# Operands kept in PSUM until they are split, upper halves on ScalarE, three norms in a row, unread matmuls, and a second product taken row by row

## The chip, the core and the metric

The kernel runs on one core of a Trainium2 chip. TensorE (PE) multiplies matrices and writes its results to PSUM, VectorE (DVE) and ScalarE (ACT) read and write SBUF and PSUM, GpSimd (POOL) works on SBUF alone, and SyncE's queue (SP) issues all the transfers of this kernel. Every engine takes its instructions in an order that is fixed when the program is built. The metric is the device time of one execution in microseconds (us); less is better.

## What is computed

For 8 sequences of 4224 positions with 192 channels, each position first gets a weighted sum of the last 7 positions, with weights from a softmax that is given per position and head (8 heads of 24 channels). Then comes the real part of a two-dimensional Fourier transform, a normalisation, and a two-layer network with 768 hidden channels:

```python
w = softmax(weight_gen, axis=-1)                      # 7 taps per position and head
u0 = sum over k of w[..., k] * x_padded[position + k] # dynamic convolution
u  = u0 + real(fft(fft(u0, axis=1), axis=2))          # mixing over positions and channels
un = (u - mean(u)) / sqrt(var(u) + 1e-6)
out = u + relu(un @ w_ch1) @ w_ch2                    # 192 -> 768 -> 192
```

The two weight matrices arrive as 64-bit floats, which the kernel reads as pairs of 32-bit words.

## The kernel before

A sequence is held as 33 rows of 128 partitions by 192 channels. It is worked off in chunks of 4 rows (8 chunks, and a ninth with the one row left), and so are its nine **groups** of the network. There are 8 x 9 = 72 groups in all. For each sequence b the steps are:

- `conv(b)` (L295): the softmax of the taps in parts (`softmax_taps`, L260; a part is two steps, advanced by `tap_step`, L284), then for each chunk seven products of x with a tap (L402 on DVE; L400 on POOL for those in `POOL_TAPS`) and their sum. The sum is taken on POOL or DVE (L411), and for the chunks in `PE_SUMS`, all in sequence 0, by PE with a unit matrix into two PSUM banks (L407), from where ACT copies it (L420). The products for PE lie in a ring of three buffers, `g2`. Rows are folded in pairs on POOL (L425, L427) and transformed over 128 points on PE (L432); the result goes by DVE (L441, L442) to DRAM, `g_d`.
- `transform(b)` (L450): `g_d` is read back (L461), transformed over the 33 rows on PE (L471), and copied by ACT to `pq` (L475 to L485).
- `mix(b, g)` (L492): the transform over the channels on PE (L500), with sums on DVE that add it to u (L506 to L510).
- `norm(b, g)` (L518): for the first three groups (`QUICK`) and the first two of sequence 1, mean and variance come from DVE (L530, L531); for the others from ACT. ACT writes the normalised rows `un` to SBUF (L551, one instruction a row), then their float16 upper half (L555). The lower half is the difference of the two, in two instructions (L557, L559), on DVE for the quick groups and on POOL otherwise. A transposing transfer makes `ht` of both halves (L562).
- `mlp(n)` (L567): a pass computes the first layer of group n, six blocks of 128 hidden channels with five matmuls each (L587), and the second layer of group n-1 (L614). The hidden values `hh` lie in a ring of ten buffers. For the first 7 groups they and w2 are float32 (L593); after that they are pairs of float16 halves (L597 on ACT, L598 on DVE). The second layer of a group fills two PSUM banks, `po`, each with two of the four rows. Before, the first half of a pass does rows 0 and 2 and the second half rows 1 and 3; at the end both banks are added to u (L621).

The weights are prepared during the opening. `prep_w1` (L232) finds a scale by powers of two (`weight_scale`, L168), makes float32 of the words in three pieces of 128 x 384 (`words_to_f32`, L193, eight DVE instructions), and splits each into float16 halves on DVE (`split_f32`, L212: the upper half L214, the lower half L215). `prep_w2(i)` (L249) does the eight instructions for the three pieces of w2, which stay float32 for now; `split_w2` (L252) splits them later. The raw words lie in the buffers that `hl`, `un` and `ht` use afterwards: the raw piece i of w2 lies in the buffer that the i-th `ht` takes.

The order of each engine is made by the planner of the language from the order in which the program is written, with a simulated time. `tc.issue_after(ins)`, used by `queue` and `behind` (L646, L663), sets further edges: an instruction on the same engine as `ins` may stand only after it. Before, the opening reads: conv(0); transform(0); the early part of conv(1), whose first two chunks are done on POOL; `prep_w1`; the first half of the last tap part of conv(1); then, for each g of 0, 1, 2: `mix`, `norm`, `prep_w2(g)`, with the second half of that tap part after the first norm's statistics. What is left of conv(1) (`rest`, L688) stands behind the last lower half of norm 2.

PSUM has 8 banks: the ring `ph` of three, `po` of two, `fft` of two and `wp` of one.

Of the kernel before, what the change touches and what calls it, by code (L numbers as in the profile page):

```python
# [11 lines left out]
F32 = mybir.dt.float32  # L12
# [26 lines left out]
F32_GROUPS = 7  # L39

# [47 lines left out]
def tile_dynconv_fnet_mlp(  # L88
# [104 lines left out]
    def words_to_f32(raw, out, nm, bank):  # L193
# [15 lines left out]
        v.scalar_tensor_tensor(out=r, in0=a, scalar=2.0 ** -49, in1=r, op0=ALU.mult, op1=ALU.mult)  # L209
        last_word.append(v.tensor_tensor(out=out, in0=w, in1=r, op=ALU.add))  # L210

    def split_f32(w, hi16, lo16, sc):  # L212

        nc.vector.tensor_scalar(out=hi16, in0=w, scalar1=sc[:, 0:1], scalar2=None, op0=ALU.mult)  # L214
        last_split.append(nc.vector.scalar_tensor_tensor(out=lo16, in0=w, scalar=sc[:, 0:1], in1=hi16,  # L215
                                                         op0=ALU.mult, op1=ALU.subtract))
# [15 lines left out]
    def prep_w1(raws):  # L232
# [3 lines left out]
        w = temp("w1f_1", F32)  # L236
        words_to_f32(raws[0], w, "w1_1", ("ph", 3))
# [57 lines left out]
    def conv(b):  # L295
# [44 lines left out]
        for grp in groups:  # L340
# [39 lines left out]
            for k in range(K):  # L380
                for c, R, u, wp, pa, wq, pt in chunks:
                    pr = u
                    if k > 0 or pa:
# [19 lines left out]
                    if pa:  # L403
                        prf = pr.rearrange("p r d -> p (r d)")
                        n = R * D // 2
                        for i in range(2):
                            nc.tensor.matmul(pa[i][:, 0:n], lhsT=ident32, rhs=prf[:, i * n:(i + 1) * n],  # L407
                                             start=(k == 0), stop=(k == K - 1))
                    elif k > 0:
                        adder = nc.vector if k <= DVE_ADDS.get((b, c), 0) else nc.gpsimd  # L410
                        adder.tensor_tensor(out=u, in0=u, in1=pr, op=ALU.add)  # L411
                yield (done + sum(q[1] for q in tails) + sum(q[1] for q in chunks) * k / K) / N2
            tails += chunks
            while tails and not (b == 1 and grp[0] == 0):
# [16 lines left out]
                for j in range(J):  # L431
                    nc.tensor.matmul(pg[:, j, :], lhsT=f1_sb[:, t2 + j, :], rhs=sm[:, j, :], start=True, stop=True)  # L432
# [8 lines left out]
                nc.vector.tensor_tensor(out=go[:, :, 1:DH - 1], in0=fwd, in1=rev, op=ALU.add)  # L441
                last_gt[b] = nc.vector.tensor_tensor(out=go[:, :, DH:D], in0=fwd, in1=rev, op=ALU.subtract)  # L442
# [5 lines left out]
                yield done / N2  # L448

# [37 lines left out]
    state, us = {}, {}  # L487
    last_product, last_fold, last_gt, last_g2, last_pp = {}, {}, {}, {}, {}
# [29 lines left out]
    def norm(b, g):  # L518
# [6 lines left out]
        un = sb.tile([P, 4, D], F32, tag="un", name=f"un_{b}_{g}", bufs=1)  # L525
        quick = NG * b + g < QUICK or (b == 1 and g < 2)
        if quick:
# [25 lines left out]
        yield 0.5  # L553
        hl = sb.tile([P, 4, 2 * D], F16, tag="hl", name=f"hl_{b}_{g}", bufs=2)
        nc.scalar.copy(hl[:, 0:T, 0:D], un[:, 0:T, :])  # L555
        lo_eng = nc.vector if quick else nc.gpsimd
        lo_eng.tensor_tensor(out=hl[:, 0:T, 2 * P:3 * P], in0=un[:, 0:T, 0:P],  # L557
                                in1=hl[:, 0:T, 0:P], op=ALU.subtract)
        last_lo[NG * b + g] = lo_eng.tensor_tensor(out=hl[:, 0:T, D:2 * P], in0=un[:, 0:T, P:D],  # L559
                                in1=hl[:, 0:T, P:D], op=ALU.subtract)  # L560
# [6 lines left out]
    def mlp(n):  # L567
# [13 lines left out]
        for c in range(NH):  # L581
# [21 lines left out]
            if last:  # L603
                s, half = divmod(c, NH // 2)
                for c2 in (2 * half, 2 * half + 1):
                    for jj in range(LJ):
                        t = 2 * jj + s
                        if t >= LT:
                            continue
# [152 lines left out]
```

## Time and profile before

| | us |
|---|---|
| median of the runs | 1173.6 (1172.6 to 1174.42, 3 runs) |
| the profiled execution: its time | 1176.11 |
| the profiled execution: its span | 1174.3 |
| granted TensorE clock over the span | 0.965 |

The span is what the instruction records cover; the time holds what lies around them as well. The idle time of a group of instructions is given with the instruction that ended it ("<-"). A granted clock of 0.5 means that PE ran at half speed.

### The profile page before, as it was taken

What the parts mean: (1) busy time and instruction counts of PE and PEld (TensorE: products, weight loads), DVE (VectorE), ACT (ScalarE), POOL (GpSimd) and SP (SyncE); (2) the same over time, 40 slices, a digit from 0 to 9 for tenths busy, and PEclk for the clock granted to TensorE, in tenths of its full rate; (3) what the DMA queues carried; (4) which work ended last, traced back from release to release, by engine and by line L of the source; (5) the groups of instructions that cost most, each with busy time, mean ns of one, the idle gap of its engine ahead of it and who ended that gap; (6) DMA issues with size and microseconds to landing.
All of it is one profiled execution on the core that took longest, in us unless ns stands there. A gap on an engine that the chain in (4) does not pass through costs nothing.

```text
span 1174.3 us, 23548 instructions
## 1 busy us (share of the span) xinstructions
PE 1087.7 (93%) x8412; PEld 823.8 (70%) x8412; DVE 1007.1 (86%) x1830; ACT 774.0 (66%) x2351; POOL 874.7 (74%) x747
## 2 busy tenths in 40 slices
PE   5776499898799999899999999899989999999998
PEld 2445277677577777688777777678767877777677
DVE  8999999789999999899989998999889996356443
ACT  1015477253798598758984699568965898589622
POOL 4869579878896999699987999699959997012200
PEclk9896699998899999999999999999999999999999
DMA  8334134531366146633474157515642224312311
GB/s 314 109 95 142 28 74 124 174 98 48 103 175 173 51 116 142 157 84 103 112 188 108 52 130 214 130 44 125 149 130 73 61 59 116 97 42 71 81 45 45
DMA packets 156501, 128.71 MB, mean 110 GB/s; under 512 B 108571, under 2 KB 133088, under 8 KB 156384
## 3 DMA queue, kind: packets, MB, share of 16 engines
q1 hardware_dynamic: 156384, 127.21, 40.3%
q8 instruction: 66, 1.08, 0.4%
q14 instruction: 51, 0.42, 0.1%
HBM read 61.46 MB, written 39.37 MB: 86 GB/s over the span
## 4 chain that ended last, share of the span: by engine, by line
PE 31%; ACT 9%; POOL 7%; issue 6%; DVE 3%; DMA 3%; SPq 0%; POOLq 0%; DVEq 0%; ACTq 0%
PE po L614 13%; PE ph L587 13%; POOL u L411 5%; PE pp L471 3%; ACT un L551 2%; ACT hh L597 2%; DMA g<-g_d 2%; ACT junk L540 2%; PE eo L500 1%; ACT junk L536 1%; DMA g_d<-gt 1%; POOL hl L557 1%; PE pg L432 1%; ACT hl L555 1%; DVE pr L402 1%
## 5 line engine op out<-in xcount | busy, mean ns | idle before, releaser
L411 POOL TENSOR_TENSOR u<-u,pr 128x768 f32<-128x768 f32 (+1 forms) x395 | 654.9, 1679 | 78.5 <-DVE pr L402 53.5
L587 PE MATMUL ph<-ht,w1h 128*128 128x512 f16 (+1 forms) x1296 | 400.1, 365 | 29.2 <-DMA ht<-hl 15.2
L614 PE MATMUL po<-w2h,hh 128*128 128x192 f16 x2832 | 408.2, 248 | 8.0 <-DVE hh L598 6.9
L614 PEld LDWEIGHTS <-hh 128*128 128x128 f16 x4248 | 364.7, 99 | 67.4 <-DVE hh L598 7.5
L402 DVE TENSOR_TENSOR pr<-x_sb,wp 128x768 f32<-128x768 f32 (+1 forms) x420 | 358.4, 876 | 16.8 <-POOL u L411 12.6
L614 PE MATMUL po<-w2l,hh 128*128 128x192 f16 x1416 | 345.6, 248 | 0.0
L598 DVE SCALAR_TENSOR_TENSOR hh<-ph,hh 128x512 f16<-128x512 f32 (+1 forms) x390 | 244.1, 633 | 112.5 <-ACT hh L597 111.5
L587 PE MATMUL ph<-ht,w1l 128*128 128x512 f16 (+1 forms) x864 | 312.0, 365 | 0.0
L597 ACT ACTIVATE hh<-ph 128x512 f16<-128x512 f32 (+1 forms) x390 | 212.7, 550 | 147.5 <-PE ph L587 146.4
L587 PEld LDWEIGHTS <-w1h 128*128 128x128 f16 x1296 | 127.1, 100 | 95.4 <-issue 5.3
L587 PEld LDWEIGHTS <-w1l 128*128 128x128 f16 x864 | 85.2, 99 | 84.2 <-issue 33.9
L551 ACT ACTIVATE un<-u,rs 128x192 f32<-128x192 f32 x264 | 123.7, 537 | 26.4 <-DVE rs L546 10.8
L557 POOL TENSOR_TENSOR hl<-un,hl 128x512 f16<-128x512 f32 (+1 forms) x67 | 72.2, 1077 | 68.3 <-ACT hl L555 44.3
L540 ACT ACTIVATE junk<-u,rs 128x192 f16<-128x192 f32 x244 | 110.5, 453 | 3.4
L536 ACT ACTIVATE junk<-u 128x192 f16<-128x192 f32 x244 | 87.7, 360 | 17.5 <-DVE u L510 14.3
L475 ACT COPY pq<-pp 97x204 f32<-97x204 f32 (+1 forms) x96 | 46.5, 485 | 60.0 <-PE pp L471 58.8
L500 PE MATMUL eo<-cs_sb,pq 97*128 97x97 f32 x544 | 80.3, 277 | 2.3 <-DVE u L510 2.2
L500 PEld LDWEIGHTS eo<-cs_sb,pq 97*128 97x128 f32 x544 | 75.2, 195 | 9.1 <-issue 1.6
L621 DVE SCALAR_TENSOR_TENSOR u<-po,isc,u 128x384 f32<-128x384 f32 (+1 forms) x122 | 69.3, 594 | 6.9 <-PE po L614 6.5
L407 PE MATMUL pa<-pr,ident 128*128 128x384 f32 x140 | 54.2, 535 | 18.3 <-DVE pr L402 15.7
L425 POOL TENSOR_TENSOR sm<-u 128x382 f32<-128x382 f32 x64 | 64.5, 1008 | 7.0 <-ACT u L420 6.8
L614 PE MATMUL po<-w2f,hh 128*128 128x192 f32 x336 | 63.9, 334 | 3.0 <-DVE u L621 3.0
(102 smaller groups left out, 1274.0 us busy)
## 6 DMA issues: line engine op xcount, KB each, us to landing
out_dram<-u SPq DMA_DIRECT2D x64, 384.0 KB
x_sb<-in_x_dram SPq DMA_DIRECT2D x48, 384.0 KB
g<-g_d SPq DMA_DIRECT2D x40, 336.0 KB
x_sb<-in_x_dram SPq DMA_DIRECT2D x8, 864.0 KB
g_d<-gt SPq DMA_DIRECT2D x32, 195.0 KB
g_d<-gt SPq DMA_DIRECT2D x32, 189.0 KB
w<-in_weight_gen_dram SPq DMA_DIRECT2D x6, 924.0 KB
x_sb<-in_x_dram SPq DMA_DIRECT2D x8, 672.0 KB
```

The lines of the kernel that those rows point to most:

```text
L402: last_product[b] = nc.vector.tensor_tensor(out=dst, in0=rows, in1=wk, op=ALU.mult)
L411: adder.tensor_tensor(out=u, in0=u, in1=pr, op=ALU.add)
L500: nc.tensor.matmul(eo[:, e, j, :], lhsT=pq[0:DH, e, r, r:r + P], rhs=cs_sb[:, e, :], start=True, stop=True)
L536: nc.scalar.activation(junk, uv[:, t, :], AF.Identity, accum_out=st[:, t, 0:1])
L540: nc.scalar.activation(junk, uv[:, t, :], AF.Square, bias=rs[:, 2, t:t + 1], accum_out=st[:, t, 1:2])
L551: nc.scalar.activation(un[:, t, :], uv[:, t, :], AF.Identity, bias=rs[:, 1, t:t + 1], scale=rs[:, 0, t:t + 1])
L557: lo_eng.tensor_tensor(out=hl[:, 0:T, 2 * P:3 * P], in0=un[:, 0:T, 0:P], in1=hl[:, 0:T, 0:P], op=ALU.subtract)
L587: last_ph[n] = nc.tensor.matmul(ph[:, 0:T], lhsT=wt[:, cs_], rhs=ht[:, 0:T, blk], start=(i == 0), stop=(i == len(terms) - 1))
L597: nc.scalar.activation(a[:, 0:T], ph[:, 0:T], AF.Relu)
L598: nc.vector.scalar_tensor_tensor(out=l[:, 0:T], in0=ph[:, 0:T], scalar=0.0, in1=a[:, 0:T], op0=ALU.max, op1=ALU.subtract)
L614: nc.tensor.matmul(po[jj][:, s, :], lhsT=hx[:, t], rhs=wx[:, c2, :], start=(c2 == 0 and i == 0), stop=(c2 == NH - 1 and i == nt - 1))
L621: nc.vector.scalar_tensor_tensor(out=lt, in0=po[jj][:, 0:m], scalar=scales[0][:, 1:2] if NG * lb + lg < F32_GROUPS else isc, in1=lt, op0=A ...
```

## The change

1. **PSUM operands.** `words_to_f32` without an `out` leaves its result in PSUM, where it was computed; `prep_w1` uses it so. `norm` of the first three groups writes `un` as two PSUM tiles of two rows each (ring `ph`), and the upper half and the difference are made per tile: two ACT and four DVE instructions in place of one and two.
2. **Upper halves on ACT.** `split_f32` makes the upper half with ACT, for w1 and, later, for w2.
3. **Order of the opening.** `prep_w2(0)` and `prep_w2(1)` are written before the first `mix`. The three pairs of `mix` and `norm` follow each other, each behind the last split of w1. `prep_w2(2)` and the second half of the tap part stand behind the last lower half of norm 1.
4. **Unread matmuls.** `keep_warm` computes into a spare bank that nobody reads: 20 float32 matmuls of 128 columns after the last fold transform of sequence 0 (ring `po`); 12 float16 ones of 384 columns after the lower half of norm 0 (ring `ph`); and 12 more, of norm 1's rows, placed at the end of pass 0 behind its first layer.
5. **Taps of POOL first.** In the chunks that PE sums, the products of POOL are taken first instead of last.
6. **Rows in sequence.** The second layer does row 0 over all six blocks, then row 1, and so on; each `po` bank is added to u as soon as its two rows are done.

```diff
@@ words_to_f32, split_f32
+        out = w if out is None else out
         last_word.append(v.tensor_tensor(out=out, in0=w, in1=r, op=ALU.add))
+        return out
...
-        nc.vector.tensor_scalar(out=hi16, in0=w, scalar1=sc[:, 0:1], scalar2=None, op0=ALU.mult)
+        nc.scalar.mul(hi16, w, sc[:, 0:1])
@@ prep_w1
-        w = temp("w1f_1", F32)
-        words_to_f32(raws[0], w, "w1_1", ("ph", 3))
+        w = words_to_f32(raws[0], None, "w1_1", ("ph", 3))
...
-            w = temp(f"w1f_0{i}", F32)
-            words_to_f32(raws[1 + i], w, f"w1_0{i}", ("ph", 3))
+            w = words_to_f32(raws[1 + i], None, f"w1_0{i}", ("ph", 3))
@@ conv
-            for k in range(K):
+            for i in range(K):
                 for c, R, u, wp, pa, wq, pt in chunks:
+                    order = [*pt, *(k for k in range(K) if k not in pt)] if pa else range(K)
+                    k = order[i]
...
+    def keep_warm(bank, nm, lhsT, rhs, count):
+
+        spare = pst(*bank, [P, 512], F32, f"warm_{nm}")
+        for _ in range(count):
+            nc.tensor.matmul(spare[:, 0:rhs.shape[-1]], lhsT=lhsT, rhs=rhs, start=True, stop=True)
@@ norm
+        if NG * b + g < QUICK:
+            halves = [pst("ph", 3, [P, 2, D], F32, f"un_{b}_{g}_{i}") for i in range(2)]
+        else:
+            un = sb.tile([P, 4, D], F32, tag="un", name=f"un_{b}_{g}", bufs=1)
+            halves = [un[:, 0:2], un[:, 2:4]]
...
-            nc.scalar.activation(un[:, t, :], uv[:, t, :], AF.Identity,
+            nc.scalar.activation(halves[t // 2][:, t % 2, :], uv[:, t, :], AF.Identity,
...
+        spans = [(un, 0, T)] if NG * b + g >= QUICK else [(h, 2 * i, 2 * i + 2) for i, h in enumerate(halves)]
+        for src, t0, t1 in spans:
+            nc.scalar.copy(hl[:, t0:t1, 0:D], src[:, 0:t1 - t0, :])
+            lo_eng.tensor_tensor(out=hl[:, t0:t1, 2 * P:3 * P], in0=src[:, 0:t1 - t0, 0:P],
+                                 in1=hl[:, t0:t1, 0:P], op=ALU.subtract)
+            last_lo[NG * b + g] = lo_eng.tensor_tensor(out=hl[:, t0:t1, D:2 * P], in0=src[:, 0:t1 - t0, P:D],
+                                                       in1=hl[:, t0:t1, P:D], op=ALU.subtract)
+        if warm:
+            keep_warm(("ph", 3), f"hl{g}", hl[:, 0, 0:P], hl[:, T - 1, 0:2 * D], WARM[2])
@@ mlp, second layer
-                s, half = divmod(c, NH // 2)
-                for c2 in (2 * half, 2 * half + 1):
-                    for jj in range(LJ):
-                        t = 2 * jj + s
...
+                for k in range(per * c, per * (c + 1)):
+                    t, c2 = divmod(k, NH)
+                    terms = ((hh[c2], w2f),) if f32 else ((hh[c2], w2h), (hh[c2], w2l), (hlo[c2], w2h))
+                    for i, (hx, wx) in enumerate(terms):
+                        nc.tensor.matmul(po[t // 2][:, t % 2, :], lhsT=hx[:, t], rhs=wx[:, c2, :],
+                                         start=(c2 == 0 and i == 0), stop=(c2 == NH - 1 and i == len(terms) - 1))
...
+                    if c2 == NH - 1 and (t % 2 == 1 or t == LT - 1):
+                        lt = lu[:, t - t % 2:t + 1]
+                        nc.vector.scalar_tensor_tensor(out=lt, in0=po[t // 2][:, 0:t % 2 + 1],
...
@@ the opening
+    with tc.issue_after(last_pg[0].ins):
+        WARM[0] and keep_warm(("po", 2), "pp", ident32, last_tile[0][:, 3, 0:P], WARM[0])
     add(0.0, 1.0, transform(0))
...
     queue(lp, (lambda n: tap_step(1, n), 5))
+    for i in range(2):
+        queue(lp, (prep_w2, i))
     for g in range(QUICK):
-        add(0.0, 1.0, behind((last_word if g else last_split)[-1].ins, mix(0, g)))
+        add(0.0, 1.0, behind(last_split[-1].ins, mix(0, g)))
         run()
         add(0.0, 1.0, norm(0, g))
         run()
-        if g == 0:
-            queue(last_bn[0, 0].ins, (lambda n: tap_step(1, n), 6))
-        queue(last_bn[0, g].ins, (prep_w2, g))
-    for i in range(QUICK, NH // 2):
-        queue(last_lo[QUICK - 1].ins, (prep_w2, i))
+    for g, call in ((1, (prep_w2, 2)), (1, (lambda n: tap_step(1, n), 6))):
+        queue(last_lo[g].ins, call)
...
+    def late_warm(g):
+        yield 0.0
+        with tc.issue_after(last_ph[g - 1].ins):
+            keep_warm(("ph", 3), f"hl{g}", hls[g][:, 0, 0:P], hls[g][:, 3, 0:2 * D], WARM[3])
...
+    add(0.93, 0.95, late_warm(1))
```

More of the change, by code (lines that the diff above doesn't have):

```diff
@@ L617, in mlp @@
-                if c == NH - 1:
-                    for jj in range(LJ):
-                        m = min(2, LT - 2 * jj)
-                        lt = lu[:, 2 * jj:2 * jj + m]
-                        nc.vector.scalar_tensor_tensor(out=lt, in0=po[jj][:, 0:m],
-                                                       scalar=scales[0][:, 1:2] if NG * lb + lg < F32_GROUPS else isc, in1=lt,
-                                                       op0=ALU.mult, op1=ALU.add)
+                f32 = NG * lb + lg < F32_GROUPS
```

43 lines of the change are left out of this document (18 added, 25 removed).

## The prediction

> **What bounds the kernel now.** First the page, for the shares of the engines over the whole span.
>
> ```profile
> span 1174.3 us, 23548 instructions
> PE 1087.7 (93%) x8412; PEld 823.8 (70%) x8412; DVE 1007.1 (86%) x1830; ACT 774.0 (66%) x2351; POOL 874.7 (74%) x747
> ```
>
> PE is busy for 93% of the span, but an average says little here. So next comes the view by stretches of time: per row the stretch and its length, then busy time (and instructions) of PE, PEld, DVE, ACT and POOL, then the granted clock.
>
> ```profile
> 0.00:76.10 76.10, 55.58 (x158) 31.13 (x159) 68.82 (x98) 9.75 (x26) 55.05 (x53) 0.96 0.55 190
> 76.10:145.40 69.30, 35.34 (x174) 25.24 (x172) 67.30 (x150) 29.87 (x79) 46.41 (x31) 0.66 0.30 82
> 145.40:180.00 34.60, 34.60 (x201) 27.17 (x200) 34.43 (x64) 26.50 (x86) 25.71 (x18) 1.00 0.30 67
> 180.00:230.00 50.00, 46.48 (x252) 37.22 (x251) 41.20 (x84) 23.41 (x71) 49.69 (x43) 0.97 0.56 167
> ...
> 320.00:1000.00 680.00, 667.22 (x5600) 511.35 (x5599) 632.11 (x1135) 532.37 (x1648) 609.92 (x527) 0.99 0.45 117
> ```
>
> From 76.1 to 145.4 DVE is busy 67.3 of 69.3 us while PE idles for half of it: this part of the opening is bound by DVE. From 145.4 to 180 DVE is still full, from 180 to 230 POOL is (49.69 of 50), and from 320 to 1000 PE has only 12.8 us of idle time in 680. The view of waits (engine and line, what it waited for, total, times, longest) says who suffers, for 76 to 160:
>
> ```profile
> POOL u L411 <- DVE u L411: 18.3, 1, 18.3
> PE ph L587 <- DMA ht<-hl: 15.2, 1, 15.2
> ```
>
> PE waits 15.2 us for the first `ht`, and POOL 18.3 us for conv(1)'s next chunk from DVE. The longest later waits of PE (from 320) and of POOL (from 145 to 1000) are these:
>
> ```profile
> PE pp L471 <- DMA g<-g_d: 8.7, 5, 2.9
> ```
>
> ```profile
> POOL u L411 <- DVE pr L402: 42.7, 14, 13.0
> ```
>
> The first is PE waiting, five times, for the transfer that follows the end of a convolution; the second is POOL waiting for DVE's products. So the convolutions, on DVE and POOL, pace the kernel from sequence to sequence, and PE fits in with little slack. What the opening is worth at the end is therefore **how much earlier DVE and POOL come to conv(1)'s remaining chunks**, not how much earlier PE starts.
>
> **The ledger of DVE.** Groups of DVE's instructions (busy time, mean ns of one), L215 to L201 from 76.1 to 107.8, L557 and L559 from 107.8 to 145.4:
>
> ```profile
> L215 DVE SCALAR_TENSOR_TENSOR w1l<-w1f,sc_w,w1h 128x384 f16<-128x384 f32 x3 | 5.4, 1806 | 0.0
> L214 DVE TENSOR_SCALAR w1h<-w1f,sc_w 128x384 f16<-128x384 f32 x3 | 4.3, 1422 | 0.0
> ...
> L201 DVE SCALAR_TENSOR_TENSOR t_w<-raw_w,pa_w 128x384 int32<-128x384 int32 x3 | 1.6, 539 | 0.0
> ...
> L557 DVE TENSOR_TENSOR hl<-un,hl 128x512 f16<-128x512 f32 x3 | 3.7, 1249 | 0.8 <-ACT hl L555 0.8
> ...
> L559 DVE TENSOR_TENSOR hl<-un,hl 128x256 f16<-128x256 f32 x3 | 3.4, 1129 | 0.0
> ```
>
> DVE's timeline where norm 2 ends and conv(1) goes on (start, duration), and POOL's restart:
>
> ```profile
> 144.42 0.69 DVE L557 TENSOR_TENSOR hl<-un,hl 128x512 f16<-128x512 f32 x1 [0.80 <-ACT hl L555]
> 145.03 0.42 DVE L559 TENSOR_TENSOR hl<-un,hl 128x256 f16<-128x256 f32 x1
> 145.36 0.39 DVE L361 TENSOR_TENSOR wp<-w,wp 128x224 f32<-128x224 f32 x1
> ```
>
> ```profile
> 152.34 5.63 POOL L411 TENSOR_TENSOR u<-u,pr 128x768 f32<-128x768 f32 x3 [18.35 <-DVE u L411]
> ```
>
> L215 takes 1806 ns; L201, of the same kind and size in the same stretch, takes 539. L201 reads one operand from PSUM, L215 both from SBUF. L557 and L559 take 0.69 and 0.42 us at 144.4, inside POOL's idle time (134.0 to 152.3), and 1249 and 1129 ns in the mean of three. So a DVE instruction with two SBUF inputs is stretched while POOL works, and one with a PSUM operand isn't. The Trainium skill ("GPSIMD Engine Reference", section 1) names two SBUF inputs, or a two-port mode, as what contends with POOL. By it `prep_w2`, most of whose operands lie in PSUM, would not be stretched where it now comes to stand beside POOL's work; the trace agrees for L201.
>
> The terms, all on the engine that binds:
> 1. **Upper halves to ACT**: three L214 go, -4.3 us. On ACT each is a copy of 384 columns out of PSUM, as this one:
>
> ```profile
> 24.22 0.48 ACT L420 COPY u<-pa 128x384 f32<-128x384 f32 x1 [0.17 <-PE pa L407]
> ```
>
> ACT is busy 29.87 of the 69.3 us. Bounds: nothing, or 3 x 0.48 = 1.4 us if ACT were the bound; I take nothing, as ACT idles for more than half.
>
> 2. **Lower halves with w in PSUM**: three L215 at L201's price, 5.4 - 3 x 0.54 = 3.8 us less.
> 3. **Differences of three norms with `un` in PSUM.** 0.69 us for 512 elements and 0.42 for 256 give 0.15 fixed and 1.05 ns an element; a norm's four halves are 2 x (0.42 + 0.28) = 1.4, and 4.2 for three against 3.7 + 3.4: 2.9 us less. Bounds: 3.8 less (three norms at the 0.69 + 0.42 of the rows), or nothing (stretched as now).
> 4. The 0.8 us of waiting ahead of L557 has `prep_w2(2)` to fill it: 0.8 less.
>
> `prep_w2` (eight instructions of L201's size, 8 x 0.54 = 4.3 us a piece) and the tap step are moved, not removed: they cost nothing in the ledger, as DVE is the bound before and after them. Sum: **-11.8 us** for the point at which DVE takes up conv(1) again (L361, 145.36), and with it for POOL's restart, 140.5 instead of 152.34. POOL's own earlier chunks end at 134.0 (152.34 - 18.35) and don't bind. From there DVE and POOL have the same work as before, and I let all of it move by 11.8 us.
>
> **PE in the opening.** SP's and PE's timeline, with the beginning of norm 1's mix on DVE:
>
> ```profile
> 122.96 1.57 SPq L562 DMA_TRANSPOSE ht<-hl  x1
> ...
> 124.00 0.36 DVE L506 TENSOR_TENSOR eo<-eo,ot 128x194 f32<-128x194 f32 x1
> ...
> 126.75 0.59 PE L587 MATMUL ph<-ht,w1h 128*128 128x512 f16 x1 [15.22 <-DMA ht<-hl]
> ...
> 134.00 12.94 SPq L562 DMA_TRANSPOSE ht<-hl  x2
> ...
> 146.84 0.38 PE L587 MATMUL ph<-ht,w1h 128*128 128x512 f16 x1
> ```
>
> The last L215 ends at 107.8. Terms 1 and 2 take 8.1 us off that and two `prep_w2` add 8.6: the first mix starts near 108.3. Norm 1 needs 10.0 us from its first L506 to its transfer; with differences of 0.7 after the last upper half in place of some 2.4, about 8.3. Then 3.8 us from issue to matmul (122.96 to 126.75): the first pass starts near 120.4, 6 us earlier. Its 30 matmuls, at 0.38 at most, end by 132, where the next pass starts at 146.84 now: PE gains some 14 us, more than DVE. The second dozen of **unread matmuls** (12 of 384 columns, at most 12 x 0.29 = 3.4 us) comes out of that surplus of 3 us and of PE's 3.5 idle us between 180 and 230: 0. The first dozen lies in the 3.8 us of the transfer and would bring the clock up (0.66 in the mean of this stretch) for a pass that isn't the bound: 0. Their banks are asked for by pass 0 or by `prep_w2` only after them.
>
> The first twenty are to speed up transform(0):
>
> ```profile
> 98.54 1.57 PE L471 MATMUL pp<-to_sb,g 102*97 102x102 f32 x8
> ...
> 103.78 0.94 PE L471 MATMUL pp<-to_sb,g 102*97 102x102 f32 x8
> ```
>
> Eight matmuls took 1.57 us with the clock down and 0.94 with it up, so each of the eleven such sets could gain up to 0.6. But the two `prep_w2` keep DVE until 108.3, past the end of the transform as it is. I take 0; bounds 0 and -5 (a planner that puts the mix ahead of `prep_w2`).
>
> **Taps of POOL first** changes no instruction of DVE, whose groups in the first 76.1 us begin so:
>
> ```profile
> L402 DVE TENSOR_TENSOR pr<-x_sb,wp 128x768 f32<-128x768 f32 (+1 forms) x54 | 44.4, 880 | 3.9 <-DMA x_sb<-in_x_dram 2.1 <-PE pa L407 1.1 <-DVE wp L361 0.5
> L361 DVE TENSOR_TENSOR wp<-w,wm 128x224 f32<-128x224 f32 x8 | 8.9, 1114 | 0.2
> ```
>
> DVE's whole wait for PE there is 1.1 us, the most that can go. Against it, PE must now have POOL's products first and the three `g2` buffers can hold DVE up, by two POOL instructions (5.63 / 3 = 1.9 us each, the row at 152.34): +3.8. I take 0, nearer to the row of DVE itself, which is full.
>
> **Rows in sequence**: the same matmuls. It loosens the wait for the sums at a pass's end, of which PE's waits over the span have this:
>
> ```profile
> PE po L614 <- DVE u L621: 3.9, 3, 3.0
> ```
>
> So -3.9 at best. Against it the last hidden block is needed a block earlier, and `hh` comes free later. I take 0; the other end is the slower rival.
>
> **Sum.** The profiled execution took 1176.11 us with a span of 1174.3, 2.5 us over the median. A span of 1162.5 would give 1164.3 for such an execution. Against the median of 1173.6 the prediction is 1173.6 - 11.8 = **1162 us**.
>
> **The rivals.**
> - *DVE finds new waits.* It now needs ACT's upper half before each lower half (three times 0.48 us and the hand-over), and of norm 2's chain of 8.3 us only what `prep_w2(2)` (4.3) and the tap step don't cover is idle. With poor cover some 5 us come back: 1167. For it: the planner's simulated time need not know of stretched instructions. Against: the cover is there. Chance 0.2.
> - *More than the ledger.* If the new order also spares DVE in the first 76 us, where L361 takes 1114 ns against 0.39 us at 145.36 (8 x 0.72 = 5.8 us), POOL's 18.3 us go nearly whole: 1156. Chance 0.12.
> - *Not the second SBUF input.* If it is the float16 output that makes L215 and the differences slow, terms 2 and 3 fail: -5.1, 1168.5. Against it stands L557 itself, with that output, at 0.69. Chance 0.05.
> - *Slower: rows in sequence starve PE.* The 72 passes from 146.84 on take 14.3 us each, 2.4 a block. The last block's hidden values were needed in the third block of the next pass and are now needed in the second, and the last two blocks find free `hh` buffers only in the last row. Where DVE is full, its half of `hh` can be later than this. It decides from 0.25 us a pass: 65 passes with float16 halves make 16 us, and 1178. For it: PE has only 12.8 us of slack in 320 to 1000. Against: the order is planned anew around it. Chance 0.1.
> - The forecast has the remaining 0.53.
>
> Faster by over 0.2% (about what a measurement of this kernel can tell from no change): the forecast and the first three rivals, less their tails, 0.85; within it 0.05; slower 0.10. The range, 1153 to 1171, holds the forecast with the bounds of its terms and the first three rivals, and leaves out the slower one.
>
> **What would show it.** L215 of w1 near 0.55 us and no L214 of w1 on DVE; the four differences of a norm near 1.4 us; the first pass near 120; POOL's restart near 140; the end of conv(1)'s sums some 12 us earlier, and from there on rows like those of before. The prediction is wrong if DVE idles between 100 and 134, if PE waits for `hh` in most passes after 320, or if the shift at 230 is gone at 1000.

## The result

The changed kernel takes 1160.1 us (median of 4 runs, 1157.28 to 1160.87), the kernel before 1173.1 us beside it (4 runs, 1170.45 to 1174.42). The ratio is 0.9883, with a 95% interval of 0.9868 to 0.9898: 13.0 us less, where 11.8 less was forecast (1162). The profiled execution of the changed kernel took 1160.23 us, that of before 1176.11, some 3 us over its median; a difference of the two traces is 15.8 us and so a little too large.

The page of the changed kernel, as the first fence of the prediction had it for the kernel before:

```profile
span 1158.5 us, 23681 instructions
PE 1085.7 (94%) x8476; PEld 819.0 (71%) x8476; DVE 987.3 (85%) x1830; ACT 776.9 (67%) x2360; POOL 873.7 (75%) x747
```

PE is busy for 2.0 us less, though it now has 64 more matmul rows (the 44 unread ones; each of the twenty float32 ones stands as two rows). It idles for 72.8 us in place of 86.6, and without the 12.4 us of unread matmuls its own work takes 14.4 us less, at a granted clock of 0.982 in place of 0.965. DVE is busy for 19.8 us less. The stretches, in the order of the prediction's table (length, then busy time of PE, PEld, DVE, ACT, POOL, then the granted clock). The first goes from DVE's arrival at w1's words to its return to conv(1) (L362, which was L361):

```profile
76.10:134.65 58.55, 36.76 (x211) 28.55 (x210) 50.98 (x146) 27.15 (x68) 44.08 (x31) 0.74 0.39 98
134.65:180.00 45.35, 45.35 (x260) 34.50 (x259) 42.92 (x80) 34.59 (x112) 35.86 (x25) 1.00 0.36 93
```

The same stretch of the kernel before ends at 145.36:

```profile
76.10:145.36 69.26, 35.30 (x173) 25.20 (x172) 67.25 (x149) 29.83 (x79) 46.41 (x31) 0.66 0.30 82
```

So DVE comes to conv(1) 10.7 us earlier. It has 16.3 us less to do until then (67.25 - 50.98), and idles for 7.6 us in place of 2.0. What it waits for stands in the groups of DVE in this stretch (busy time, mean ns | idle time ahead of the group):

```profile
L574 DVE TENSOR_TENSOR hl<-un,hl 128x256 f16<-128x256 f32 x6 | 2.5, 418 | 1.4 <-ACT hl L573 1.2
L218 DVE SCALAR_TENSOR_TENSOR w1l<-pw_w,sc_w,w1h 128x384 f16<-128x384 f32 x3 | 1.8, 614 | 5.3 <-ACT w1h L217 5.3
L576 DVE TENSOR_TENSOR hl<-un,hl 128x128 f16<-128x128 f32 x6 | 1.7, 279 | 0.0
```

The lower halves of w1 take 614 ns in place of 1806, the differences of three norms 2.5 + 1.7 = 4.2 us in place of 7.1, and the three L214 are gone from DVE. But DVE now waits 5.3 us for ACT's upper halves. ACT's timeline shows why (start, duration):

```profile
102.70 0.52 ACT L485 COPY pq<-pp 97x204 f32<-97x204 f32 x1 [0.35 <-PE pp L481]
103.01 0.55 ACT L490 COPY pq<-pp 97x204 f32<-97x204 f32 x1
103.36 0.57 ACT L217 ACTIVATE w1h<-pw_w,sc_w 128x384 f16<-128x384 f32 x1
103.82 0.52 ACT L485 COPY pq<-pp 97x204 f32<-97x204 f32 x1
```

ACT isn't busy, but its instructions run in order: L217 stands behind copies that wait for PE's transform. The idle share of an engine doesn't say that it will be free when one needs it.

PE's and POOL's timelines at the places that the prediction named:

```profile
125.18 4.00 PE L458 MATMUL warm_hl<-hl 128*128 128x384 f16 x12 [10.24 <-DVE rs L557]
129.89 0.39 PE L607 MATMUL ph<-ht,w1h 128*128 128x512 f16 x1 [0.71 <-DMA ht<-hl]
...
138.94 2.12 PE L458 MATMUL warm_hl<-hl 128*128 128x384 f16 x12
140.89 0.38 PE L607 MATMUL ph<-ht,w1h 128*128 128x512 f16 x1
```

```profile
143.74 10.02 POOL L414 TENSOR_TENSOR u<-u,pr 128x768 f32<-128x768 f32 x5 [10.53 <-DVE u L414]
```

The first pass starts 3.1 us **later** than before (129.89 against 126.75), but then runs at the full clock (0.39 us where it was 0.59), and the second starts 5.9 us earlier (140.89 against 146.84). POOL goes on 8.6 us earlier, 2.1 us less than DVE's return to conv(1) would give. What this leads to is seen where transform(1) begins, that is, where conv(1) is through; in the kernel before and in the changed one:

```profile
246.97 0.86 PE L471 MATMUL pp<-te_sb,g 102*97 102x102 f32 x8
```

```profile
234.72 0.91 PE L481 MATMUL pp<-te_sb,g 102*97 102x102 f32 x8 [1.01 <-DMA g<-g_d]
```

That is 12.3 us earlier. The 15.8 us between the two traces are these 12.3, then 1.6 lost up to the beginning of transform(7) (756.7 us before, 758.3 after), and 5.1 won from there to the end (170.6 and 165.5). The 5.1 are for the most part work done ahead of that mark: when transform(7) begins, PE has issued 1775 of its 2160 first-layer (`ph`) matmuls in the changed kernel and 1765 before, and behind it PE is busy for 162.5 us in place of 167.1.

### The profile page after: what moved, and what is told of

The parts are those of the page before. It is cut to its first block, busy times and chain, and to the rows that moved or that the text cites. A ratio compares the mean times of both kernels' runs of the same rounds, so it can differ in the third digit from the quotient of the medians.

```text
span 1158.5 us, 23681 instructions
## 1 busy us (share of the span) xinstructions
PE 1085.7 (94%) x8476; PEld 819.0 (71%) x8476; DVE 987.3 (85%) x1830; ACT 776.9 (67%) x2360; POOL 873.7 (75%) x747
## 5 line engine op out<-in xcount | busy, mean ns | idle before, releaser
L414 POOL TENSOR_TENSOR u<-u,pr 128x768 f32<-128x768 f32 (+1 forms) x395 | 655.7, 1679 | 67.4 <-DVE pr L405 51.5
L630 PE MATMUL po<-w2h,hh 128*128 128x192 f16 x2832 | 416.2, 246 | 5.6 <-DVE hh L618 4.3
L405 DVE TENSOR_TENSOR pr<-x_sb,wp 128x768 f32<-128x768 f32 (+1 forms) x420 | 357.3, 873 | 13.1 <-POOL u L414 10.2
L565 ACT ACTIVATE un<-u,rs 128x192 f32<-128x192 f32 x264 | 123.9, 536 | 23.1 <-POOL rs L563 9.8
L635 DVE SCALAR_TENSOR_TENSOR u<-po,isc,u 128x384 f32<-128x384 f32 (+1 forms) x122 | 72.3, 592 | 5.0 <-PE po L630 4.9
L410 PE MATMUL pa<-pr,ident 128*128 128x384 f32 x140 | 53.2, 520 | 21.0 <-POOL pr L403 11.8
L563 POOL TENSOR_TENSOR rs<-rs 128x4 f32<-128x4 f32 (+1 forms) x61 | 12.1, 200 | 68.3 <-ACT hh L617 38.8
```

The lines of the kernel that those rows point to most:

```text
L405: last_product[b] = nc.vector.tensor_tensor(out=dst, in0=rows, in1=wk, op=ALU.mult)
L565: nc.scalar.activation(halves[t // 2][:, t % 2, :], uv[:, t, :], AF.Identity, bias=rs[:, 1, t:t + 1], scale=rs[:, 0, t:t + 1])
L630: nc.tensor.matmul(po[t // 2][:, t % 2, :], lhsT=hx[:, t], rhs=wx[:, c2, :], start=(c2 == 0 and i == 0), stop=(c2 == NH - 1 and i == len(t ...
L635: nc.vector.scalar_tensor_tensor(out=lt, in0=po[t // 2][:, 0:t % 2 + 1], scalar=scales[0][:, 1:2] if f32 else isc, in1=lt, op0=ALU.mult, o ...
```

## The experiments

Theory D, the prediction's: DVE and POOL pace the kernel from conv(1) on, so the gain is what the ledger of DVE gives. Its rivals changed as runs came in: that the sums in sequence or the new order of the opening bring the gain; that PE paces instead (theory P); and that the order in which the planner puts the later instructions decides. For the order of all instructions is planned anew for each kernel: a small edit of the opening puts a fifth to three tenths of DVE's 1830 instructions in another place, up to the end. (Counted are those that fall outside the longest order that two traces have in common; the expectations below say half and a third, which was too much.)

All runs in one table. Ratios are to runs of the kernel before that were made beside each kernel (their median lay between 1172.0 and 1173.1 us), so kernels of different rounds are better compared by the ratios. The columns: median; ratio to the kernel before, with its 95% interval; and, from the one profiled execution of each, the start of DVE's first weights for conv(1) behind the norms (L361 in before), the start of transform(1), the length from there to transform(7), and from there to the end.

| kernel | us | ratio (interval) | conv(1) | transform(1) | to transform(7) | to the end |
|---|---|---|---|---|---|---|
| before | 1173.1 | | 145.36 | 247.0 | 756.7 | 170.6 |
| after | 1160.1 | 0.9883 (0.9868 to 0.9898) | 134.65 | 234.7 | 758.3 | 165.5 |
| ledger alone | 1180.0 | 1.0068 (1.0055 to 1.0081) | 139.51 | 246.1 | 760.7 | 170.8 |
| sums in sequence alone | 1170.9 | 0.9989 (0.9978 to 1.0) | 145.76 | 247.0 | 756.6 | 165.2 |
| after, ledger undone | 1165.4 | 0.9947 (0.9933 to 0.9962) | 139.88 | 241.4 | 757.7 | 165.4 |
| after, nothing unread | 1162.1 | 0.9916 (0.99 to 0.9933) | 133.12 | 234.5 | 758.4 | 165.5 |
| after, DVE loaded | 1173.0 | 1.0 (0.9985 to 1.0016) | 146.99 | 247.4 | 761.4 | 165.5 |
| after, PE loaded | 1191.7 | 1.0171 (1.0143 to 1.0198) | 134.02 | 235.3 | 789.0 | 165.5 |
| after, upper halves on DVE | 1168.3 | 0.9958 (0.9943 to 0.9973) | 131.44 | 231.5 | 769.5 | 165.8 |
| after, old order | 1196.2 | 1.0195 (1.0167 to 1.0223) | 136.56 | 240.1 | 788.2 | 165.5 |
| after, one unread matmul less | 1161.3 | 0.9906 (0.9891 to 0.9922) | 135.90 | 236.8 | 761.2 | 165.5 |
| upper halves on DVE, no second dozen | 1156.5 | 0.9858 (0.9839 to 0.9878) | 130.62 | 233.1 | 750.2 | 165.4 |
| after, no second dozen | 1159.8 | 0.9885 (0.9863 to 0.9906) | 133.48 | 235.9 | 756.3 | 165.6 |
| upper halves on DVE, second dozen of 11 | 1159.8 | 0.9891 (0.9864 to 0.9918) | 131.12 | 231.2 | 759.0 | 165.3 |

The last four columns come from single executions, and these lay up to 6 us from the median of their kernel: 3 us over it for before and the DVE load, 4.0 over it for one unread matmul less, 6.0 under it for upper halves on DVE without the second dozen. So differences of a few us in the last two columns are not yet differences of the kernels.

### The parts by themselves

**The ledger alone**: the kernel before with the upper halves on ACT, and words and normalised rows in PSUM.

```
-        nc.vector.tensor_scalar(out=hi16, in0=w, scalar1=sc[:, 0:1], scalar2=None, op0=ALU.mult)
+        nc.scalar.mul(hi16, w, sc[:, 0:1])
...
-            words_to_f32(raws[1 + i], w, f"w1_0{i}", ("ph", 3))
+            w = words_to_f32(raws[1 + i], None, f"w1_0{i}", ("ph", 3))
...
+            halves = [pst("ph", 3, [P, 2, D], F32, f"un_{b}_{g}_{i}") for i in range(2)]
```

> The kernel before, with only the three edits of DVE's ledger (upper halves on ACT, words of w1 and normalised rows of the first three norms in PSUM); order of the opening, taps, sums and no unread matmuls as before. Theory (the gain is what DVE's ledger gives conv(1)): about -11.8, 1161 us, first conv(1) L361 row some 11 us earlier than 145.36. Rival 'rows': some 4 to 5 us of the gain come from the sums in sequence, at the kernel's end: 1165 to 1166. Rival 'order': without the new order of the opening DVE waits for ACT's upper halves and for the chain of norm 2, and half of the gain is missing: 1167.

Measured: 1180.0 us, **slower** than before by 8 us. All the times that were expected fall, the theory's first; the rival 'order' had the wait for ACT, but 1167. Its edits do on DVE what they should (lower halves of 614 ns, as in the changed kernel), but the stretch up to conv(1) reads so:

```profile
L217 DVE SCALAR_TENSOR_TENSOR w1l<-pw_w,sc_w,w1h 128x384 f16<-128x384 f32 x3 | 1.8, 614 | 8.5 <-ACT w1h L216 8.5
```

```profile
130.83 0.61 PE L593 MATMUL ph<-ht,w1h 128*128 128x512 f16 x1 [18.15 <-DVE hl L565]
...
138.65 0.61 PE L593 MATMUL ph<-ht,w1h 128*128 128x512 f16 x1 [5.51 <-DVE hl L565]
```

DVE waits 8.5 us for the three upper halves. PE stands for 18.15 us, does five matmuls, and stands again, so the second pass starts at 148.3 where the kernel before has 146.84. Both waits end 0.06 us after a norm's last difference on DVE (L565). That difference reads `un`, which now lies in the ring `ph`, and the first layer asks for buffers of the same ring of three. So with the old order, where norms 1 and 2 stand beside pass 0, the ledger makes PE wait for DVE. (The trace shows the releaser and the code the ring; no run gave `un` other buffers.) conv(1) comes back 5.9 us earlier, and transform(1) only 0.9: the head start is lost in between, and the stretch to transform(7) then takes 4.0 us more than in the trace of before. An earlier conv(1) alone is not worth its size.

**The sums in sequence alone**: the kernel before with the new loop over `po`.

```
+                for k in range(per * c, per * (c + 1)):
+                    t, c2 = divmod(k, NH)
```

> The kernel before, with only the sums row after row. Theory: nothing, 1173 us within 0.2%. Rival 'rows': 1168 to 1169, with the last stretch (behind the last convolution) some 4 us shorter. The slower rival of the prediction: 1178 or more.

Measured: 1170.9 us, ratio 0.9989 (0.9978 to 1.0): at most 2.6 us, the theory's "nothing" within its bound. Yet the table has the stretch behind transform(7) at 165.2 to 165.8 in every kernel with the new loop and at 170.6 and 170.8 in the two without it. So the loop does move some 5 us of work out of the end, as the rival has it, but that is not a gain of 5 us: by transform(7) PE has issued 1775 `ph` matmuls with the new loop and 1765 without it. The two traces differ by 5.5 us all the same. That of before is of an execution 3 us over its median, with a granted clock of 0.984 on the way from transform(1) to transform(7) where this kernel has 0.991 (stretches at half speed worth some 12 and 7 us), so the times are the better measure. No run has the changed kernel with the old loop; beside the ledger and the new order the loop may be worth another amount.

**The ledger undone** in the changed kernel, for w1 and the first three norms; the rest stays.

```
+            nc.vector.tensor_scalar(out=hi16, in0=w, scalar1=sc[:, 0:1], scalar2=None, op0=ALU.mult)
...
+        w = words_to_f32(raws[0], temp("w1f_1", F32), "w1_1", ("ph", 3))
...
+            un = sb.tile([P, 4, D], F32, tag="un", name=f"un_{b}_{g}", bufs=1)
```

> The kernel after, with the three edits of the ledger undone for w1 and the first three norms (upper halves on DVE, words and normalised rows in SBUF); new order, unread matmuls, taps and sums in sequence stay. Theory: the gain is gone, 1172 us, and lower halves and differences take 1.7 us and over 1.1 us again. Rival 'rows': 1168. Rival 'order' (the order of the opening is what pays): 1165 or less.

Measured: 1165.4 us. The theory (1172) fails and the rival 'order' (1165 or less) is met to 0.4 us. It is the cleanest of these comparisons: only 112 of DVE's 1830 instructions stand elsewhere than in the changed kernel, and the later stretches agree within 0.6 us. The ledger is worth 5.3 us here by the medians (1165.4 - 1160.1), 7.5 by the ratios and 6.7 at transform(1), and not 11.8; the rest came with the other parts. DVE's groups up to conv(1):

```profile
L580 DVE TENSOR_TENSOR hl<-un,hl 128x128 f16<-128x128 f32 x6 | 6.5, 1080 | 0.0
L578 DVE TENSOR_TENSOR hl<-un,hl 128x256 f16<-128x256 f32 x6 | 6.1, 1021 | 1.2 <-ACT hl L577 1.2
L221 DVE SCALAR_TENSOR_TENSOR w1l<-w1f,sc_w,w1h 128x384 f16<-128x384 f32 x3 | 4.7, 1581 | 0.0
L218 DVE TENSOR_SCALAR w1h<-w1f,sc_w 128x384 f16<-128x384 f32 x3 | 1.5, 494 | 0.0
```

With SBUF operands the differences take 12.6 us in place of 4.2 and the lower halves 4.7 in place of 1.8. The upper halves cost 1.5 on DVE, and no wait.

**Without the 44 unread matmuls**: `WARM = (0, 0, 0, 0)`.

> The kernel after without any of the 44 unread matmuls. Theory: within 0.2% of 1160 us, since PE in the opening isn't what binds. Rival 'clock': the unread matmuls pay by a faster transform and first pass, so without them 1163 to 1165. Other side: the second dozen costs PE 2.1 us in front of pass 1, so without it 1158.

Measured: 1162.1 us (0.9916, 0.99 to 0.9933), against 0.9883 (0.9868 to 0.9898): 2.0 us slower by the medians and 3.9 by the ratios, whose intervals lie just apart. In the traces the spans are equal (1158.4 and 1158.5 us): PE is spared the 12.4 us of the unread groups (6.3 and 6.1 in the changed kernel), idles for 6.8 us more in all, and runs at a lower clock (0.973 against 0.982). That is near the upper edge of the theory's 0.2% by the medians, and the rival's 3 to 5 us by the ratios. As 482 of DVE's instructions also stand elsewhere, this run doesn't settle whether the unread matmuls pay; transform(1) starts at 234.5 without them and at 234.7 with them.

### Who paces

**DVE loaded**: seven DVE additions of 128x768 behind norm 2's last difference, ahead of conv(1).

```
+            spent.append(nc.vector.tensor_tensor(out=t.rearrange("p r d -> p (r d)"),
+                                                 in0=f1_sb[:, 0:6, :].rearrange("p t k -> p (t k)"),
+                                                 in1=f1_sb[:, 6:12, :].rearrange("p t k -> p (t k)"), op=ALU.add))
...
+    queue(last_lo[QUICK - 1].ins, (dve_load, 7))
```

> The kernel after with seven more DVE additions of 128x768 (0.94 us each, 6.6 us, their result unread) between norm 2's last difference and conv(1)'s remaining chunks. Theory D (the prediction's: DVE and POOL pace the kernel from conv(1) on): 1166 to 1167 us, and conv(1)'s L362 and POOL's restart some 6.6 us later. Theory P (PE paces it: what counts is how long PE idles up to pass 1, as 34.0 us of idle time before and 21.8 after between 76 us and pass 1, and 36.6 in the ledger alone): within 1.5 us of 1160.

**PE loaded**: `WARM = (20, 0, 12, 46)`, 34 more unread matmuls ahead of pass 1.

> The kernel after with 34 more unread matmuls of 384 columns ahead of pass 1 (46 in place of 12; 0.177 us each by the 2.12 us of the twelve, so 6.0 us of PE alone). Theory P: 1166 us, all of it paid at the end. Theory D: 1160 to 1161, since PE has the surplus of some 3 us there and the 10.5 us that POOL waits.

Measured: 1173.0 and 1191.7 us. Neither theory has these times: D forecast 1166 to 1167 and 1160 to 1161, P within 1.5 us of 1160 and 1166. At transform(1) the answer is clear: the load on DVE comes out there in full and more (247.4, 12.7 later; conv(1) comes back 12.3 later, since the planner let the mixes 3 and 4 and the rest of w2's words go ahead of it), the load on PE hardly at all (235.3, 0.6 later). **Up to transform(1) theory D holds for these two loads** (the ledger alone, whose earlier conv(1) didn't come through, stands against it). Behind it, it doesn't: the kernel with the PE load needs 789.0 us to transform(7) where 758.3 was the time. The two rows for that stretch, of the changed kernel and of the loaded one, and whom PE waited for in the loaded one:

```profile
234.72:993.00 758.28, 734.11 (x6128) 561.93 (x6129) 700.27 (x1268) 573.66 (x1773) 677.53 (x575) 0.99 0.43 113
```

```profile
235.30:1024.30 789.00, 750.06 (x6166) 570.14 (x6166) 707.06 (x1272) 572.54 (x1776) 679.24 (x575) 0.98 0.41 109
```

```profile
PE po L630 <- DVE hh L618: 11.0, 3, 5.7
PE ph L607 <- DVE hh L618: 9.6, 14, 2.2
```

PE is busy for 95 to 97% of this stretch, so what it has left at transform(1) it must still do. At that point the changed kernel has issued 205 of its `ph` matmuls (30 to a pass), the loaded one 185, two thirds of a pass less: 20 of 30, at 14.2 us a pass (767.2 us for the 54 passes from 9 to 63 in the changed kernel) some 9.5 us. That is a good half of the 16 us by which PE is busier. The other 15 are waits, among them 20.6 us for DVE's `hh` in place of 4.3 + 2.3, at a granted clock of 0.98 against 0.99. So **behind transform(1) PE paces, as theory P has it**, as far as these shares can tell. But a fivefold price for 6 us of load is neither theory's; that the later order fell badly too would explain it, and isn't shown.

**The old order** with all other parts: norms one behind the other.

```
+        if g == 0:
+            queue(last_bn[0, 0].ins, (lambda n: tap_step(1, n), 6))
+        queue(last_bn[0, g].ins, (prep_w2, g))
```

> The kernel after with the opening's order of before (each norm behind the one ahead of it, one w2 piece of words behind each norm's statistics); ledger, unread matmuls, taps and sums in sequence stay. Theory P: pass 1 starts some 7 us later, as in the ledger alone (148.3 against 140.9), less 5 us that the sums in sequence took off the last stretch in the profiles: 1168 to 1173. Theory D: conv(1)'s L362 at 139.5 as in the ledger alone, 4.9 later than after: 1165.

Measured: 1196.2 us, far off both. PE meets the same two waits in its first pass as with the ledger alone:

```profile
127.88 0.61 PE L607 MATMUL ph<-ht,w1h 128*128 128x512 f16 x1 [6.70 <-DVE hl L576]
...
135.79 0.58 PE L607 MATMUL ph<-ht,w1h 128*128 128x512 f16 x1 [5.61 <-DVE hl L576]
```

Neither the changed kernel nor the one with the ledger undone has a wait of the first layer for these differences, nor has the kernel before. So the new order, with three norms ahead of pass 0, is what makes room for `un` in the ring. transform(1) starts at 240.1, with 185 `ph` matmuls issued, as in the kernel with the PE load, and the stretch to transform(7) is as bad (788.2 us, PE waiting 24.4 us for `hh`). Both, and the ledger alone (190), are kernels in which PE is behind at transform(1); the kernel before had issued 210 by then. So the order of the opening pays by 5.4 us at transform(1), and PE comes there with more of its work done. How much the latter decides is open: the ledger alone, with 190, needed only 4.0 us more than before up to transform(7). Why DVE is late with `hh` in the two bad orders was not found.

### The wait that came in, and the luck of the order

**Upper halves on DVE**, read from PSUM, all else as changed.

```
+        if dve:
+            nc.vector.tensor_scalar(out=hi16, in0=w, scalar1=sc[:, 0:1], scalar2=None, op0=ALU.mult)
```

> The kernel after with the upper halves of w1 on DVE again, out of PSUM (three instructions, 0.35 to 0.72 us each in the run without the ledger); so DVE doesn't wait for ACT, which has them behind the transform's copies (5.3 us in the kernel after). Both theories: +1.5 -5.3 = -3.8, 1156 to 1157 us, first pass and conv(1) some 3.8 us earlier. If the wait only moves (DVE then waits for PE's transform, whose end at 107.2 the first mix needs): 1159 to 1160.

Measured: the opening does as expected (conv(1) 3.2 us earlier, transform(1) 231.5, 3.2 earlier), the time doesn't: 1168.3 us, 8 slower than the changed kernel. All of it is lost behind transform(1) (769.5 us against 758.3).

**One unread matmul less** ahead of pass 0, `WARM = (20, 0, 11, 12)`: no edit of substance, but 410 of DVE's 1830 instructions come to stand elsewhere.

> The kernel after with eleven in place of twelve unread matmuls ahead of pass 0: 0.2 us of PE's work in a place where PE waits for the transfer anyway, but the order of about half of DVE's instructions comes out another way, as in the runs with the loads. Theory 'mechanism' (an edit is worth what it does at its place): within 1 us of 1160. Theory 'order' (what comes behind conv(1) hangs on how the planned order happens to fall): opening as in the kernel after (transform(1)'s first matmul near 234.7, within 1.5 us), but the 758 us from there to transform(7) come out between 756 and 790, and the time with it anywhere from 1158 to 1190.

Measured: 1161.3 us (0.9906, 0.9891 to 0.9922). That is near the theory of the mechanism and within the wide range of the other: a new order alone moved the time by 1.2 us (some 2.7 by the ratios), not by 20. transform(1) comes 2.0 us later, where the second theory allows 1.5.

**Upper halves on DVE and no second dozen**: both edits, `WARM = (20, 0, 12, 0)`.

> The kernel after with the upper halves of w1 on DVE (opening some 3 us earlier, as transform(1) at 231.5 against 234.7 showed) and without the second dozen of unread matmuls (2.1 us of PE). Theory 'mechanism': 1160.1 - 3.2 - 2.1 = 1155. Theory 'order': transform(1) starts at 231 to 232, and the end is 1155 only if the stretch up to transform(7) takes 758 us as in the kernel after; at 770 to 790 it is 1167 to 1187.

Measured: 1156.5 us, ratio 0.9858 (0.9839 to 0.9878), the lowest of all, though its interval overlaps that of the changed kernel. (Its profiled execution, 1150.5 us, was its fastest by 5.9 us, so the 750.2 us in the table flatter it.) DVE's stretch up to conv(1):

```profile
75.90:130.62 54.72, 34.23 (x208) 26.20 (x207) 51.66 (x149) 25.08 (x64) 43.10 (x29) 0.78 0.41 104
```

```profile
L218 DVE TENSOR_SCALAR w1h<-pw_w,sc_w 128x384 f16<-128x384 f32 x3 | 1.8, 588 | 0.0
```

DVE's idle time falls from 7.6 to 3.1 us for 1.8 us of work.

**No second dozen alone**, and **the second dozen cut to eleven with the upper halves on DVE** (`WARM = (20, 0, 12, 11)`):

> The kernel after without the second dozen of unread matmuls alone (upper halves stay on ACT). Theory 'mechanism': the dozen takes 2.1 us of PE right behind pass 0, where PE has no idle time to spare: 1158, pass 1 at 138.8 in place of 140.9. By the prediction (it comes out of a surplus of PE): 1160. Theory 'order': transform(1) at 234.7 within 1.5 us, the end anywhere from 1157 to 1190.

> The run with the upper halves on DVE (1168 us, against 1156.5 for the same without the second dozen) with eleven in place of twelve in that dozen: 0.18 us of PE's work less, but about a third of DVE's instructions stand in another order. Theory 'order': that run lost its 3.8 us gain to the order behind transform(1), and another order gives 1155 to 1158. Theory 'mechanism' (the second dozen costs this much when the opening is early): 1167 to 1168.5 again.

Measured: 1159.8 us each. Without the second dozen nothing changes by itself, as the prediction had it and not as the mechanism theory had it: pass 1 starts 3.1 us earlier, transform(1) 1.2 later. And one unread matmul less turns 1168.3 into 1159.8, with the same opening (transform(1) at 231.2 for 231.5) and the stretch to transform(7) at 759.0 for 769.5. The median lies between what the two theories forecast (1155 to 1158, and 1167 to 1168.5), and its executions fall into two groups, three at 1156.7 to 1157.3 and three at 1162.3 to 1165.1; all six are faster than the 1165.4 to 1170.4 of the kernel with twelve. So the 8 us that the upper halves on DVE lost were the later order's, not the halves'. Across these orders the scatter is some 3 us and once 8, and the old order and the PE load lost some 20 to 30 us behind transform(1) in ways not found; a difference of 3 us between two such kernels can't be put down to the edit that was made.

## Why the prediction was right, and where not

The time was right, and so was the place up to transform(1). The shift at conv(1) was forecast at 11.8 us and came out at 10.7, at transform(1) 12.3, at the end 13.0. **Its make-up was not**, and by one of the prediction's own signs it was wrong: DVE idles for 6.7 us between 100 and 134, where it idled for 0.7 before.

- **Term 1 (upper halves to ACT, -4.3) failed.** The three instructions went, but the wait for ACT that the first rival priced at some 5 us came in, at 5.3. The step took ACT's idle share for its being free; ACT's copies of the transform run in order ahead of L217, and they wait for PE. What it should have weighed is a halves' price on DVE out of PSUM: 1.8 us, with no wait. The rival's mechanism was right for the upper halves, and wrong about norm 2's chain: DVE waited 1.4 us ahead of the differences.
- **Terms 2 and 3 (PSUM operands) hold**: 5.4 to 1.8 us, forecast 1.6, and 7.1 to 4.2, forecast 4.2. With the ledger undone the cost is back (4.7 and 12.6). The rival "not the second SBUF input" falls with it. **Term 4** (0.8 us) held for norm 2, whose wait is gone, but 1.2 us came in ahead of norm 1's differences, so the three norms wait for 1.4 us in all. The rule that the prediction drew (two SBUF inputs) leaves out L214, which has one SBUF input beside its scalar and took 1422 ns all the same.
- **"Moved, not removed, nothing in the ledger" failed, to the good.** DVE's busy time up to conv(1) fell by 16.3 us: 4.3 + 3.6 + 2.9 of the ledger, and 5.5 more. Some 4.5 of these are four of the eight instructions of the last w2 piece (2.2 us) and three of the fourth mix (1.5), which now stand behind L362, and an L414 that is stretched less (1.3 us in place of 2.1). It made up for the wait of term 1: two wrong terms of about 5 us, with opposite signs, lie under the right sum. That is luck.
- **POOL's restart near 140** failed: 143.74, 8.6 us earlier. The work moved behind L362 isn't free there: between L362 and the DVE sum for which POOL waits (L414) stand 2.6 us of mix and words, where the kernel before had 0.4. The rest of the 12.3 us at transform(1) was won behind the restart, where POOL's next long wait for DVE is 10.2 us in place of 13.0; the prediction had nothing for it.
- **The first pass near 120.4 failed**: 129.9. The prediction gave the first norm the 10.0 us that norm 1 took by itself; the planner runs two norms side by side, and the first is not through before 125. PE gains 5.9 us by pass 1, not 14.
- **Unread matmuls**: forecast 0. The second dozen is worth nothing (0.9885 without it), as forecast; without all 44 the kernel was 2.0 to 3.9 us slower, which may be the order.
- **Taps of POOL first**: forecast 0. DVE comes to w1's exponents (L176) at 76.85 us in the changed kernel and at 75.89 to 76.14 in the runs without unread matmuls, with the old order or with the best edit, against 76.10 before. It wasn't tried by itself.
- **Rows in sequence**: forecast 0. Alone the loop gives 0 to 2.6 us; beside the other parts it wasn't tried.
- **"DVE and POOL pace the kernel, PE fits in with little slack"** holds up to transform(1), by the two loads, and fails behind it. There the end follows what PE still has to do and how long it waits. In the changed kernel PE came along (205 `ph` matmuls against 210 before), and the shift at conv(1) went through. The prediction had no such condition; that it is the one that decides is argued, not shown.
- **The slower rival** (sums in sequence starve PE) did not happen: PE's waits for DVE's `hh` are 4.3 + 2.3 us in the long stretch, and the loop alone is no slower. **More than the ledger** (DVE spared in the first 76 us) didn't either.

So the forecast was right by its sum, with luck. That the ledger, beside the other parts, is the cause is shown for 5 to 7.5 us of the 13. The rest came with the other parts, which without the ledger give 5.6 us at transform(1) (241.4 against 247.0); the order of the opening is the likeliest of them, since taking it back costs 5.4 us there, but the taps were never tried alone. The parts don't add up one by one: the ledger alone makes the kernel slower, and with the old order it makes PE wait for the ring `ph`.

## What to carry to other kernels

Work given to an idle engine comes back when that engine's queue lets it, so price the queue ahead of it (here 5.3 us) and not the engine's free share. A buffer that an operand keeps in a shared ring is taken from the ring's other users: here, with the ledger alone, PE stood for 5.51 us in its first pass until a norm let go of `ph`. Check a saving on the binding engine against the next one: the two kernels in which PE came to transform(1) with the least done lost the most behind it. Where a planner sets the order, try an edit that does nothing before reading a difference of a few us.

## What the runs showed of the hardware

- The stretching of a DVE instruction with two SBUF operands beside POOL's work does not go by its size. In the kernel with the ledger undone, differences of 128x128 took 1080 ns in the mean and those of 128x256 took 1021; out of PSUM they take 279 and 418. The means mix two cases: the third norm's four stand in POOL's idle time and take 0.41, 0.28, 0.40 and 0.27 us, and of the eight beside POOL's work seven take 1.08 to 1.89 us and one 0.41. Cutting such instructions in two more than doubles the loss: beside POOL's work the cut differences of two norms took 11.2 us, the whole ones of the kernel before 6.0, and without POOL they take some 2.7 and 2.2.
- It is POOL, not SBUF alone: the same lower half, for w2 and with both inputs in SBUF, took 0.61 us in the kernel before while POOL stood idle (L215, three in a row; POOL's next instruction below, after 12.99 us of waiting). L214, with one SBUF input, took 0.41 us there and 1422 ns in the mean for w1:

```profile
231.50 1.07 DVE L214 TENSOR_SCALAR w2h<-w2f,sc_w 128x384 f16<-128x384 f32 x3
...
232.56 1.67 DVE L215 SCALAR_TENSOR_TENSOR w2l<-w2f,sc_w,w2h 128x384 f16<-128x384 f32 x3
```

```profile
242.84 3.72 POOL L411 TENSOR_TENSOR u<-u,pr 128x768 f32<-128x768 f32 x2 [12.99 <-DVE pr L402]
```

  The Trainium skill ("GPSIMD Engine Reference", section 1) names two SBUF inputs beside POOL's work as what contends; for L215 the runs agree, with 1806 ns beside POOL's work and 0.61 us without it.
- The granted clock fell again in the middle of the transform in the changed kernel: it was 1.0 from 88.7 us, after the unread matmuls, to 95.5, and then 0.5 to 102.4. PE had idled for 2.1 of the last 6.8 us before it fell. Only two sets of eight ran at the full clock:

```profile
93.18 0.91 PE L481 MATMUL pp<-te_sb,g 102*97 102x102 f32 x8 [1.52 <-DMA g<-g_d]
93.93 0.86 PE L481 MATMUL pp<-to_sb,g 102*97 102x102 f32 x8
95.40 1.57 PE L481 MATMUL pp<-te_sb,g 102*97 102x102 f32 x8 [0.61 <-ACT pq L495]
96.77 1.57 PE L481 MATMUL pp<-to_sb,g 102*97 102x102 f32 x8
```
